# A newly written order of all engines for a windowed attention and rational MoE kernel on one core

## The chip, the core and the metric

The kernel runs on one core of one Trainium2 chip. The metric is the device time of one execution in microseconds (us), lower is better. Runs of the same kernel on one chip agree within some 0.3%.

## The reference, cut to what matters

Attention over 8 batches and 8 heads of 576 positions (head size 64) with two masks, and behind it a two-layer network whose activation is a quotient of polynomials:

```python
mask_plain = (rel >= 0) & (rel < window)
mask_dil = (rel >= 0) & (rel < window * dilation) & (rel % dilation == 0)
...
scores = np.where(masks[None, :, :, :], scores, -1000000000.0)
scores = scores - np.max(scores, axis=-1, keepdims=True)
attn = np.exp(scores)
attn = attn / (np.sum(attn, axis=-1, keepdims=True) + 1e-09)
return np.matmul(attn, v).astype(np.float32)
...
h = x @ w_in
P = a[0] + a[1] * h + a[2] * h2 + a[3] * h3
Q = 1.0 + np.abs(b[0]) * np.abs(h) + np.abs(b[1]) * h2
g = P / (Q + 1e-06)
return (g @ w_out).astype(np.float32)
```

There are 4608 tokens of width 512 and 2048 hidden units, all in float32.

## The kernel before, in words

The attention is cut into 48 units of six per batch (`Unit`, U0 to U47), the network into tiles (`Tile`, T0 to T111, and from T112 on `QuadTile`): a tile is 128 hidden units (f) by 512 tokens (a column block c). What the tensor engine multiplies is held as a high and a low float32r part.

**A unit** does its scores on PE; then on DVE mask, maximum and subtraction, on ACT the exponential, on DVE a 32x32 transposition (`turn`, L561). From there it goes through memory: SP issues `put` (L575, the profile's turned<-u), waits until that has landed, and issues `move` (L569, two transfers, the profile's pT<-turned). Then one step on PE, the unit's use (the profile's pair), multiplies by v and does the scores of the unit two further on. The loads of qk and v are issued by SP too. The results are normed and turned on DVE (`turn_out`) and become the high and low parts xh and xl of a block's tokens; the last 64 tokens of each batch go to memory instead (left<-y).

**A tile** is one step h on PE (12 matmuls into one of two PSUM banks; 4 full float32 ones for T0 to T5), a chain (`plan_chain`, L1029) of three ACT steps on h, a product a<-r,a called qq (L1037, DVE or POOL), two DVE steps t1 and t2, ln and exp on ACT, three DVE steps g0, g1, g2, then the high part gh (L1050: ACT, DVE or POOL) and the low part gl (L1051: DVE or POOL), and four steps out on PE of three matmuls each. The bank is free when g2 is done, so h of a tile waits for g2 of the tile two before it.

**Sums and Mix** prepare the last two column blocks, which are multiplied with seven products in place of eight (`Quad`). `Mix.fetch` (L1389, the profile's left<-left) reads what the units' left<-y wrote to memory, and `Mix.one` (L1400, the profile's t<-left,xh) is the first that uses it.

**The order is written out by hand.** Each piece of work is an operation with a number. `Plan.run` (L324) walks through the list ISSUE (L78) and emits the operations in that order; an operation goes to the engine that the table ENGINE (L236) gives for its number, and without an entry to the first engine that it allows. The list holds 3929 steps, and each engine has its own steps in the list's order: PE 813, DVE 1279, ACT 1017, POOL 434, SP 386. An engine never passes a step that waits. In the list a unit's turn, put, move and use have the numbers 534, 535, 536, 555 for U22, and 424, 425, 426, 445 for U15.

Of the kernel before, what the change touches and what calls it, by code (L numbers as in the profile page):

```python
# [97 lines left out]
    1144, 1145, 204, 197, 406, 1142, 407, 1143, 408, 1147, 1146, 409, 1148, 1155, 1132, 203, 1156, 1157, 1158, 1159, 1162, 1163, 1160, 1161, 1164,
    1117, 1115, 1116, 205, 1165, 1166, 209, 1080, 238, 240, 159, 239, 241, 1078, 1118, 1133, 1149, 1150, 206, 1173, 1174, 1175, 1177, 1135, 1136,
    1134, 1176, 227, 400, 1178, 199, 1179, 228, 1167, 1168, 1180, 1181, 1183, 1182, 1184, 229, 200, 201, 1191, 1192, 1194, 1193, 1151, 1152, 1154,  # L100
    1153, 1209, 1169, 1172, 1171, 1170, 401, 1196, 211, 244, 274, 220, 262, 232, 410, 1195, 246, 242, 1185, 1186, 1198, 1199, 1197, 1201, 1200, 1202,
    222, 1210, 234, 1211, 1212, 1213, 1216, 1217, 1214, 1215, 1218, 1219, 1220, 230, 207, 1203, 212, 1204, 1227, 245, 221, 1187, 1190, 1228, 1230,
    1229, 252, 233, 223, 1231, 1232, 247, 213, 1189, 1188, 1221, 1222, 1234, 1235, 1233, 1236, 1237, 1245, 248, 251, 1246, 1247, 1248, 1249, 253, 235,
    1238, 236, 224, 254, 1207, 1205, 1206, 1208, 1263, 1226, 1224, 1223, 1250, 1239, 1252, 1253, 225, 237, 231, 1240, 255, 276, 243, 1251, 1255, 1254,
    1256, 412, 427, 256, 280, 268, 398, 396, 411, 1225, 1244, 1242, 1281, 1243, 1241, 269, 1264, 1266, 257, 1265, 1257, 1268, 1267, 263, 1270, 1271,
    1269, 1258, 258, 264, 1282, 1284, 281, 1273, 1272, 259, 265, 1274, 1275, 270, 1276, 1261, 1259, 1260, 1299, 1262, 1278, 1279, 1283, 275, 282,
    1285, 249, 1288, 1289, 260, 1286, 1287, 1291, 1290, 1302, 1300, 1301, 1304, 1292, 1305, 1293, 1294, 271, 261, 1303, 1306, 1307, 1277, 1280, 1317,
    1297, 1298, 1295, 1296, 1309, 1308, 1310, 266, 1318, 1320, 1319, 1322, 1321, 1323, 267, 1335, 1311, 1312, 1324, 1325, 272, 277, 278, 273, 1327,
    1326, 1328, 1314, 1316, 1315, 1353, 1313, 1336, 1337, 1338, 1329, 402, 1339, 1342, 1343, 1330, 279, 1340, 1341, 1344, 1345, 1346, 1354, 1355,
    1347, 403, 1356, 1357, 283, 284, 1360, 414, 1331, 415, 420, 416, 1358, 1348, 1359, 421, 417, 422, 1361, 1363, 1362, 1332, 1379, 1380, 1334, 1333,  # L110
    429, 1351, 1382, 423, 418, 1384, 1364, 424, 1381, 1383, 1386, 1387, 436, 1385, 430, 1388, 1389, 1365, 1366, 285, 1397, 1350, 1349, 1352, 1368,
    1370, 1369, 1398, 1400, 1399, 1401, 1404, 419, 404, 431, 1390, 432, 433, 1377, 1405, 1391, 1402, 1403, 437, 434, 1392, 1367, 1415, 1373, 1375,
    1371, 438, 1406, 1407, 1408, 443, 435, 439, 1416, 1417, 1418, 413, 425, 426, 445, 440, 452, 453, 1376, 454, 428, 441, 442, 1378, 444, 1394, 1393,
    1395, 1396, 1433, 1420, 1419, 446, 1409, 455, 456, 1421, 1410, 1422, 1423, 1424, 1425, 1426, 1436, 1434, 1435, 1438, 447, 1427, 1414, 1412, 1411,
    1437, 1440, 1441, 1439, 448, 1442, 1443, 1444, 1372, 1428, 1413, 1451, 1432, 1430, 1431, 457, 458, 1374, 459, 475, 451, 1452, 1454, 1456, 1457,
    461, 1429, 468, 462, 1469, 1453, 1455, 1445, 1458, 1459, 1460, 1446, 1461, 1462, 1463, 1464, 1470, 1472, 1471, 449, 469, 463, 464, 1473, 1476,
    1477, 470, 1474, 1475, 1479, 1478, 1480, 1450, 1447, 1449, 1448, 1487, 1466, 477, 1465, 1468, 1505, 1467, 1488, 1489, 1481, 471, 1491, 1490, 1494,
    465, 1495, 1482, 450, 466, 1483, 1485, 478, 479, 480, 484, 472, 1492, 1493, 481, 1496, 1508, 1506, 485, 1497, 1498, 486, 1484, 1486, 473, 1523,
    474, 491, 460, 1526, 467, 1529, 1507, 1510, 1509, 1512, 1513, 1499, 1511, 1514, 1500, 1515, 482, 1535, 493, 1538, 1536, 1537, 1539, 1503, 1502,
    1501, 1516, 1517, 499, 500, 1540, 1518, 1541, 1542, 1543, 1544, 1553, 1504, 501, 1545, 494, 1521, 1519, 1556, 1554, 502, 1555, 1557, 1520, 1558,  # L120
    1546, 1524, 1522, 1527, 1559, 1530, 1571, 1547, 1548, 1532, 476, 1528, 1533, 495, 1525, 492, 506, 1531, 483, 1560, 487, 1561, 521, 1550, 1551,
# [1542 lines left out]
```

## Time and profile before

| | |
|---|---|
| Median of 3 runs | 930.32 us (929.02 to 931.96) |
| The profiled execution | 929.68 us, its span 927.9 us |
| Granted clock of PE over the span | 0.985 |
| PE, DVE, ACT, POOL busy | 95%, 87%, 70%, 54% |

The profile names an instruction by line, engine and tiles (out<-in). Almost all are issued by small helpers, so that the line tells little and the tiles tell the work. PE is the tensor engine's matmuls, DVE the vector engine, ACT the scalar engine, POOL the GpSimd engine, SP the queue that issues the transfers.

### The profile page before, as it was taken

The numbers are of one execution on the slowest core, as the hardware profiler recorded it, in microseconds if no ns is written. First come the engines' busy times: TensorE is split into PE (matmuls) and PEld (weight loads), VectorE is DVE, ScalarE is ACT, GpSimd is POOL, SyncE is SP. The second block draws the span as 40 slices with busy tenths as digits, with TensorE's granted clock in tenths as the row PEclk, the third lists the DMA queues.
The fourth block names the chain that finished last, engine by engine and source line by source line (L and its number), as shares of the span: only waits on it lengthen the run. The fifth ranks groups of instructions, "written<-read, shape, count | busy, mean of one in ns | idle before, by whom it ended". The sixth has DMA issues, their size and how long they took to land.

```text
span 927.9 us, 20345 instructions
## 1 busy us (share of the span) xinstructions
PE 879.9 (95%) x7788; PEld 690.8 (74%) x7788; DVE 809.8 (87%) x1447; ACT 651.5 (70%) x1042; POOL 503.4 (54%) x460
## 2 busy tenths in 40 slices
PE   8799998989999999899799999999897999999998
PEld 6346876867777787787678887877685888877786
DVE  6899997988988799889788799899987889999886
ACT  5698897755677566656577676766775778988761
POOL 3476876732445434257567654576773665544650
PEclk9899999999999999999899999999999999999999
DMA  9988550034353433234564066117563035355023
GB/s 336 282 264 278 181 201 0 16 81 118 119 176 88 116 114 115 80 111 123 144 194 146 1 191 189 35 40 239 161 181 109 1 103 147 125 174 186 5 91 137
DMA packets 93634, 125.20 MB, mean 135 GB/s; under 512 B 39648, under 2 KB 64864, under 8 KB 93024
## 3 DMA queue, kind: packets, MB, share of 16 engines
q1 hardware_dynamic: 93248, 123.80, 42.2%
q8 instruction: 61, 1.00, 0.4%
q14 instruction: 37, 0.30, 0.1%
q10 hardware_dynamic: 288, 0.10, 0.1%
HBM read 86.25 MB, written 37.62 MB: 133 GB/s over the span
## 4 chain that ended last, share of the span: by engine, by line
PE 45%; DVE 24%; DMA 10%; ACT 8%; issue 6%; POOL 4%; SPq 2%; DVEq 0%; POOLq 0%; ACTq 0%
PE out L367 21%; PE h L367 14%; ACT r L370 5%; DVE h L376 4%; DVE a L376 4%; PE pair L367 3%; SPq L364 2%; DMA turned<-u 2%; PE hy L367 2%; DMA pT<-turned 2%; DVE t L373 2%; PE hz L367 2%; PE hx L367 2%; DVE a L373 2%; DMA qk<-in_qk_dram 2%
## 5 line engine op out<-in xcount | busy, mean ns | idle before, releaser
L367 PE MATMUL out<-gh,wo 128*128 128x512 f32 x1104 | 346.7, 395 | 0.0
L367 PE MATMUL h<-xh,wi 128*128 128x512 f32 x848 | 284.4, 396 | 12.6 <-DVE a L376 12.1
L367 PEld LDWEIGHTS out<-gh,wo 128*128 128x128 f32 x1104 | 206.8, 190 | 44.9 <-ACT os L370 0.7
L367 PE MATMUL out<-gl,wo 128*128 128x512 f32 x552 | 216.7, 393 | 1.0 <-POOL gl L379 0.9
L367 PEld LDWEIGHTS h<-xh,wi 128*128 128x128 f32 x848 | 160.2, 189 | 55.0 <-DVE a L376 19.7
L379 POOL TENSOR_TENSOR a<-r,a 128x512 f32<-128x512 f32 x68 | 89.5, 1316 | 177.6 <-ACT r L370 157.0
L367 PE MATMUL h<-xl,wi 128*128 128x512 f32 x424 | 166.0, 391 | 0.0
L379 POOL TENSOR_TENSOR gl<-a,gh 128x512 fp32r<-128x512 f32 x92 | 125.1, 1360 | 36.7 <-DVE gh L382 19.6
L370 ACT ACTIVATE r<-a,ln_bias 128x512 f32<-128x512 f32 x112 | 80.8, 722 | 76.1 <-POOL a L379 42.0
L367 PEld LDWEIGHTS out<-gl,wo 128*128 128x128 f32 x552 | 104.6, 189 | 24.3 <-POOL gl L379 2.1
L370 ACT ACTIVATE t<-h,na_t 128x512 f32<-128x512 f32 x112 | 86.1, 769 | 30.2 <-PE h L367 27.4
L370 ACT ACTIVATE r<-r,exp_bias 128x512 f32<-128x512 f32 x144 | 104.0, 722 | 4.1
L370 ACT ACTIVATE r<-a,ab_t 128x512 f32<-128x512 f32 x112 | 91.2, 814 | 21.3 <-DVE a L376 14.1
L370 ACT ACTIVATE a<-h 128x512 f32<-128x512 f32 x112 | 66.3, 592 | 53.4 <-PE h L367 42.0
L376 DVE SCALAR_TENSOR_TENSOR h<-h,na_t,r 128x512 f32<-128x512 f32 x112 | 84.1, 751 | 16.4 <-ACT r L370 15.0
L373 DVE TENSOR_TENSOR t<-t,h 128x512 f32<-128x512 f32 x112 | 75.8, 676 | 24.8 <-ACT t L370 14.8
L376 DVE SCALAR_TENSOR_TENSOR a<-a,r 128x512 f32<-128x512 f32 x112 | 88.4, 790 | 7.1 <-ACT r L370 6.0
L367 PEld LDWEIGHTS h<-xl,wi 128*128 128x128 f32 x424 | 80.2, 189 | 16.2 <-issue 0.5
L376 DVE SCALAR_TENSOR_TENSOR h<-t,na_t,h 128x512 f32<-128x512 f32 x112 | 83.7, 748 | 1.9
L376 DVE SCALAR_TENSOR_TENSOR a<-a,h 128x512 f32<-128x512 f32 x106 | 72.1, 680 | 2.6
L391 POOL TENSOR_SCALAR gh<-a 128x512 fp32r<-128x512 f32 x37 | 27.1, 733 | 56.3 <-PE out L367 29.6
L379 POOL TENSOR_TENSOR place<-r,place 128x512 f32<-128x512 f32 x26 | 35.0, 1351 | 39.9 <-ACT r L370 39.1
(207 smaller groups left out, 1361.5 us busy)
## 6 DMA issues: line engine op xcount, KB each, us to landing
qk<-in_qk_dram SPq DMA_DIRECT2D x48, 448.0 KB, 4.8
v<-in_vp_dram SPq DMA_DIRECT2D x48, 390.0 KB, 4.3
out_dram<-os SPq DMA_DIRECT2D x36, 256.0 KB, 3.0
wi_raw<-in_w_in_dram SPq DMA_DIRECT2D x16, 512.0 KB, 5.3
wo_raw<-in_w_out_dram SPq DMA_DIRECT2D x16, 512.0 KB, 6.0
turned<-u SPq DMA_DIRECT2D x42, 192.0 KB, 2.1
pT<-turned SPq DMA_DIRECT2D x84, 96.0 KB, 2.7
sums<-wi SPq DMA_DIRECT2D x24, 256.0 KB, 3.0
```

The costliest lines, as they stand in the source:

```text
L364: pin((nc.scalar if eng == "ACT" else nc.sync).dma_start(dst, src))
L367: pin(nc.tensor.matmul(o, lhs, rhs, start=start, stop=stop, skip_group_check=skip))
L370: pin(nc.scalar.activation(o, i, func, **kw))
L373: pin(nc.vector.tensor_tensor(o, x, y, op))
L376: pin(nc.vector.scalar_tensor_tensor(o, x, s, y, op0, op1))
L379: pin(nc.gpsimd.tensor_tensor(o, x, y, op))
L391: pin(nc.gpsimd.tensor_scalar(o, x, 1.0, 0.0, ALU.mult, ALU.add))
```

## The change

The first 240 steps of ISSUE stay as they are (the last PE step among them is h of T3, at 49 us of the span). From there on the 3689 others stand in a new order, on every engine. No operation is added or taken away. Of those that stand on the same engine before and after, 606 of PE's 813 have another place in PE's order (by 1.8 places in the mean, 18 at most), and 301 of SP's 386 (2.6 and 12).

The table ENGINE names another engine for 259 operations. Two of these, 0 and 3, have no effect: their functions pass the queue "ACT" themselves (L1220, L1238). Of the 257 others 72 go from DVE to POOL, 69 from POOL to DVE, 41 from ACT to POOL, 32 from POOL to ACT, 26 from DVE to ACT and 17 from ACT to DVE. Of the products qq, 28 come to DVE and 18 leave it; of the low parts gl, 10 come and 18 leave.

The core of the diff: the lines with U22's turn, put, move and use, those with the first step of Mix (3138), and two of ENGINE's.

```diff
@@ -83,206 +83,209 @@
...
-    1654, 1655, 1662, 1664, 1663, 1665, 1668, 1669, 1666, 540, 546, 1667, 541, 542, 1656, 1679, 1640, 1641, 543, 1680, 1682, 1658, 1671, 1670, 1672,
-    534, 528, 544, 547, 1673, 1681, 1683, 1659, 1697, 1674, 1684, 548, 549, 550, 1685, 1686, 1687, 1688, 522, 538, 545, 553, 535, 536, 569, 1689, 555,
...
-    2806, 2826, 2807, 2824, 2828, 2829, 2830, 2831, 3138, 2834, 2835, 2832, 2833, 2836, 2837, 2838, 3139, 3137, 3145, 3140, 2846, 2848, 3142, 2847,
...
+    529, 1635, 1636, 528, 532, 1622, 1623, 520, 1646, 1645, 1648, 1624, 1661, 1621, 533, 1637, 1647, 534, 1649, 1638, 1650, 1651, 1640, 1639, 1662,
+    1664, 1653, 1652, 1654, 1663, 1665, 539, 1666, 1655, 1668, 1667, 535, 522, 553, 536, 569, 1656, 1669, 1679, 1641, 1642, 546, 547, 540, 541, 542,
+    1670, 1682, 543, 1680, 545, 1658, 1671, 544, 1672, 1657, 1673, 1684, 1685, 1697, 1681, 1674, 1683, 548, 549, 550, 1675, 1700, 1698, 1686, 1687,
+    1676, 1660, 555, 1659, 1678, 1677, 1702, 551, 538, 1689, 1688, 1690, 1699, 1715, 1701, 1691, 562, 563, 556, 557, 1704, 1705, 564, 565, 1703, 1706,
...
+    941, 2832, 2833, 934, 2837, 2836, 2838, 942, 3135, 3136, 2846, 2847, 2848, 2849, 2852, 2853, 2850, 2851, 2839, 2840, 2855, 3138, 2854, 2856, 2863,
...
 ENGINE = {
-    12: "ACT", 24: "ACT", 36: "ACT", 49: "ACT", 55: "ACT", 63: "ACT", 69: "ACT", 78: "ACT", 84: "DVE", 86: "ACT", 87: "DVE", 88: "ACT", 89: "DVE",
...
+    0: "SP", 3: "SP", 12: "ACT", 24: "ACT", 36: "ACT", 49: "ACT", 55: "ACT", 63: "ACT", 69: "ACT", 78: "ACT", 84: "DVE", 86: "ACT", 87: "DVE",
```

What the lists put between a unit's put and its use can be counted. The table gives the PE steps that stand in the list between the step that lets SP issue the put (the unit's turn, or, where that stands later, the step on another engine that an earlier entry of SP's queue waits for) and the use. "out0" is an out of T0 to T5, with full float32 matmuls.

| Unit | before | after |
|---|---|---|
| U15 | 1 h, 1 out | 1 h, 7 out |
| U18 | 1 h, 2 out | 3 h, 11 out, 1 use |
| U19 | 1 h, 4 out | 3 h, 9 out |
| U22 | 1 h, 1 out | 2 h, 9 out, 1 use |
| U29 | 1 h, 3 out | 2 h, 7 out |
| U33 | 5 out | 1 h, 5 out, 1 use |
| U35 | 1 h, 5 out | 2 h, 8 out |
| U39 | 1 h, 5 out | 2 h, 9 out, 1 use |
| U11 | 2 h, 7 out0, 1 use | 1 h, 2 out0, 1 use |
| U20 | 2 h, 6 out, 1 use | 1 h, 5 out |
| U27 | 3 h, 10 out, 1 use | 1 h, 5 out |
| U45 | 2 h, 7 out | 2 h, 10 out |

In DVE's order the first step of Mix (3138) stands 5 steps behind turn_out of U47 before and ahead of t1, t2, g0, g1 and g2 of T102 (2832 to 2838); after, it stands 13 steps behind that turn_out, behind all of T102's steps, and ahead of g0 and g2 of T103 (2854, 2856).

## Rows read from the trace of the kernel before

**Rows 1.** The page's first part: busy time and share by engine.
```profile
PE 879.9 (95%) x7788; PEld 690.8 (74%) x7788; DVE 809.8 (87%) x1447; ACT 651.5 (70%) x1042; POOL 503.4 (54%) x460
```

**Rows 2.** Windows from 50 us: PE, PEld, DVE, ACT, POOL busy; clock, DMA share, GB/s.
```profile
50.00:125.00 75.00, 74.50 (x814) 49.41 (x813) 72.93 (x138) 65.16 (x110) 57.50 (x51) 1.00 0.78 261
125.00:200.00 75.00, 71.16 (x490) 57.02 (x489) 67.58 (x108) 59.03 (x95) 51.69 (x45) 1.00 0.11 28
200.00:450.00 250.00, 236.52 (x2633) 190.15 (x2632) 218.31 (x417) 158.72 (x252) 109.72 (x101) 0.98 0.39 114
450.00:475.00 25.00, 19.74 (x261) 15.55 (x260) 17.84 (x39) 14.51 (x26) 10.49 (x11) 0.86 0.73 221
475.00:650.00 175.00, 174.01 (x1572) 140.72 (x1570) 155.15 (x280) 121.90 (x191) 110.07 (x97) 1.00 0.40 122
650.00:690.00 40.00, 37.02 (x429) 29.30 (x429) 37.32 (x75) 29.73 (x49) 30.50 (x30) 1.00 0.52 165
690.00:725.00 35.00, 28.55 (x119) 22.83 (x119) 25.89 (x40) 22.61 (x34) 15.84 (x13) 0.95 0.37 107
725.00:900.00 175.00, 173.60 (x761) 141.86 (x760) 158.25 (x236) 142.97 (x224) 94.09 (x79) 1.00 0.34 110
```

**Rows 3.** Waits of PE from 50 us on: us in total, times, longest.
```profile
PE pair L367 <- DMA pT<-turned: 12.4, 8, 4.9
PE h L367 <- DVE a L376: 12.1, 11, 4.8
PE pair L367 <- DMA qk<-in_qk_dram: 3.0, 2, 2.1
PE pair L367 <- DMA v<-in_vp_dram: 2.2, 2, 1.4
```

**Rows 4.** The window behind U33's wait, columns as in the windows above.
```profile
462.00:464.00 2.00, 2.00 (x73) 1.64 (x61) 0.90 (x3) 0.00 (x0) 0.00 (x0) 0.50 0.77 235
```

**Rows 5.** The page's DMA issues: count, KB each, median us to landing.
```profile
qk<-in_qk_dram SPq DMA_DIRECT2D x48, 448.0 KB, 4.8
...
turned<-u SPq DMA_DIRECT2D x42, 192.0 KB, 2.1
pT<-turned SPq DMA_DIRECT2D x84, 96.0 KB, 2.7
```

**Rows 6.** The chain in order of time, steady stretches of PE: start, us, what.
```profile
45.73 3.43 PE out L367 x8
...
168.40 2.72 PE h L367 x12
171.12 2.72 PE out L367 x12
```

**Rows 7.** PE's timeline, a unit's use (pair) and the step behind it.
```profile
188.70 0.67 PE L367 MATMUL pair<-v,pT 64*32 64x65 f32 x44
...
189.83 0.73 PE L367 MATMUL out<-gh,wo 128*128 128x512 f32 x2
```

**Rows 8.** Timelines of DVE and SP about the first step of Mix.
```profile
692.78 0.68 DVE L373 TENSOR_TENSOR a<-r,a 128x512 f32<-128x512 f32 x1
699.33 0.69 DVE L373 TENSOR_TENSOR t<-left,xh 128x512 f32<-128x512 f32 x1 [5.87 <-DMA sums<-wi]
...
690.04 0.88 SPq L364 DMA_DIRECT2D left<-y  x2
...
693.36 0.81 SPq L364 DMA_DIRECT2D left<-left  x2
```

**Rows 9.** Groups of DVE and POOL: count, busy us, mean ns, idle before.
```profile
L376 DVE SCALAR_TENSOR_TENSOR a<-a,r 128x512 f32<-128x512 f32 x112 | 88.4, 790 | 7.1 <-ACT r L370 6.0 <-POOL gl L379 1.1
...
L376 DVE SCALAR_TENSOR_TENSOR a<-a,h 128x512 f32<-128x512 f32 x106 | 72.1, 680 | 2.6
L373 DVE TENSOR_TENSOR a<-r,a 128x512 f32<-128x512 f32 x44 | 38.2, 868 | 5.6 <-ACT r L370 5.1 <-POOL wo L379 0.4
...
L379 POOL TENSOR_TENSOR a<-r,a 128x512 f32<-128x512 f32 x68 | 89.5, 1316 | 177.6 <-ACT r L370 157.0 <-DVE t L373 12.8 <-PE pair L367 5.2
```

More of the change, by code (lines that the diff above doesn't have):

```diff
@@ new lines @@
+    108: "POOL", 110: "POOL", 111: "POOL", 114: "ACT", 116: "POOL", 117: "POOL", 120: "ACT", 122: "ACT", 123: "POOL", 126: "POOL", 128: "POOL",
+    129: "DVE", 132: "POOL", 134: "ACT", 135: "DVE", 138: "POOL", 140: "ACT", 141: "POOL", 144: "ACT", 146: "POOL", 147: "POOL", 150: "ACT",
+    152: "POOL", 153: "DVE", 156: "POOL", 158: "ACT", 159: "POOL", 162: "ACT", 164: "ACT", 165: "POOL", 168: "POOL", 170: "DVE", 171: "POOL",
+    174: "POOL", 176: "ACT", 177: "POOL", 180: "POOL", 182: "ACT", 183: "POOL", 186: "ACT", 188: "ACT", 189: "POOL", 192: "ACT", 194: "ACT",
@@ new lines @@
+    195: "POOL", 198: "ACT", 200: "POOL", 201: "POOL", 204: "POOL", 206: "POOL", 207: "POOL", 210: "POOL", 212: "ACT", 213: "DVE", 216: "POOL",
+    218: "ACT", 219: "POOL", 222: "ACT", 224: "ACT", 225: "POOL", 228: "ACT", 230: "ACT", 231: "POOL", 234: "POOL", 236: "POOL", 237: "POOL",
+    240: "POOL", 242: "POOL", 243: "POOL", 246: "ACT", 248: "ACT", 249: "DVE", 252: "POOL", 254: "DVE", 255: "POOL", 258: "POOL", 260: "DVE",
+    261: "DVE", 264: "ACT", 266: "POOL", 267: "POOL", 270: "POOL", 272: "ACT", 273: "DVE", 276: "ACT", 278: "ACT", 279: "POOL", 282: "ACT",
@@ new lines @@
+    284: "POOL", 285: "POOL", 312: "DVE", 327: "POOL", 342: "POOL", 388: "DVE", 404: "DVE", 419: "POOL", 434: "POOL", 466: "POOL", 498: "DVE",
+    513: "POOL", 528: "DVE", 560: "POOL", 592: "DVE", 607: "POOL", 622: "POOL", 654: "DVE", 670: "DVE", 686: "POOL", 701: "POOL", 716: "POOL",
+    780: "POOL", 795: "POOL", 810: "DVE", 826: "POOL", 874: "POOL", 889: "POOL", 904: "POOL", 934: "DVE", 947: "DVE", 963: "POOL", 979: "POOL",
+    995: "POOL", 1011: "POOL", 1027: "DVE", 1043: "POOL", 1051: "ACT", 1052: "POOL", 1061: "POOL", 1069: "POOL", 1070: "POOL", 1075: "ACT",
@@ new lines @@
+    1077: "DVE", 1079: "ACT", 1081: "ACT", 1087: "DVE", 1095: "DVE", 1096: "POOL", 1105: "DVE", 1113: "POOL", 1114: "POOL", 1123: "DVE", 1131: "ACT",
+    1132: "POOL", 1141: "DVE", 1149: "ACT", 1150: "POOL", 1159: "DVE", 1167: "ACT", 1168: "POOL", 1177: "DVE", 1185: "ACT", 1186: "POOL", 1195: "DVE",
+    1203: "POOL", 1204: "POOL", 1213: "DVE", 1221: "POOL", 1222: "POOL", 1231: "DVE", 1239: "ACT", 1240: "POOL", 1249: "DVE", 1257: "ACT",
+    1258: "DVE", 1267: "DVE", 1275: "POOL", 1276: "POOL", 1285: "POOL", 1293: "POOL", 1294: "POOL", 1303: "POOL", 1311: "POOL", 1312: "POOL",
@@ new lines @@
+    1321: "DVE", 1329: "ACT", 1330: "POOL", 1339: "DVE", 1347: "ACT", 1348: "POOL", 1357: "POOL", 1365: "POOL", 1366: "POOL", 1371: "ACT",
+    1373: "ACT", 1375: "ACT", 1377: "ACT", 1383: "POOL", 1391: "ACT", 1392: "DVE", 1401: "POOL", 1409: "POOL", 1410: "POOL", 1419: "DVE", 1427: "DVE",
+    1428: "POOL", 1437: "POOL", 1445: "POOL", 1446: "POOL", 1455: "POOL", 1463: "ACT", 1464: "POOL", 1473: "POOL", 1481: "POOL", 1482: "POOL",
+    1491: "POOL", 1499: "POOL", 1500: "POOL", 1509: "POOL", 1517: "DVE", 1518: "POOL", 1539: "POOL", 1547: "POOL", 1548: "POOL", 1557: "POOL",
@@ new lines @@
+    1565: "DVE", 1566: "POOL", 1575: "POOL", 1583: "DVE", 1584: "POOL", 1593: "DVE", 1601: "ACT", 1602: "POOL", 1619: "POOL", 1709: "DVE",
+    1710: "DVE", 1719: "POOL", 1727: "ACT", 1737: "POOL", 1745: "POOL", 1763: "POOL", 1764: "POOL", 1781: "POOL", 1791: "DVE", 1799: "POOL",
+    1817: "ACT", 1823: "ACT", 1825: "ACT", 1827: "DVE", 1829: "ACT", 1843: "DVE", 1853: "DVE", 1861: "ACT", 1879: "POOL", 1880: "DVE", 1897: "DVE",
+    1915: "POOL", 1925: "DVE", 1933: "POOL", 1943: "DVE", 1951: "POOL", 1961: "DVE", 1969: "POOL", 1979: "DVE", 1987: "DVE", 1988: "POOL",
@@ new lines @@
+    3056: "POOL", 3060: "DVE", 3061: "POOL", 3062: "POOL", 3063: "POOL", 3064: "POOL", 3065: "POOL", 3066: "DVE", 3067: "POOL", 3070: "POOL",
+    3071: "POOL", 3075: "POOL", 3076: "POOL", 3077: "POOL", 3078: "POOL", 3079: "POOL", 3080: "DVE", 3081: "ACT", 3082: "POOL", 3085: "ACT",
+    3086: "POOL", 3090: "POOL", 3091: "DVE", 3092: "POOL", 3093: "DVE", 3094: "POOL", 3095: "DVE", 3096: "POOL", 3097: "POOL", 3100: "DVE",
+    3101: "POOL", 3105: "POOL", 3106: "POOL", 3107: "POOL", 3108: "POOL", 3109: "POOL", 3110: "POOL", 3111: "POOL", 3112: "POOL", 3115: "POOL",
@@ new lines @@
+    3116: "DVE", 3120: "POOL", 3121: "POOL", 3122: "POOL", 3123: "DVE", 3124: "POOL", 3125: "POOL", 3126: "ACT", 3127: "POOL", 3130: "ACT",
+    3131: "DVE", 3138: "DVE", 3139: "POOL", 3140: "ACT", 3141: "POOL", 3142: "ACT", 3143: "POOL", 3144: "DVE", 3145: "DVE", 3146: "ACT", 3147: "DVE",
+    3148: "ACT", 3149: "POOL", 3150: "POOL", 3151: "POOL", 3152: "POOL", 3153: "DVE", 3157: "DVE", 3158: "POOL", 3159: "ACT", 3160: "DVE",
+    3161: "POOL", 3162: "DVE", 3163: "POOL", 3164: "POOL", 3165: "POOL", 3166: "DVE", 3167: "POOL", 3168: "DVE", 3169: "POOL", 3170: "POOL",
@@ new lines @@
+    3171: "ACT", 3172: "POOL", 3214: "POOL", 3240: "POOL", 3281: "POOL", 3307: "POOL", 3308: "DVE", 3337: "POOL", 3350: "POOL", 3376: "POOL",
+    3377: "DVE", 3404: "POOL", 3405: "POOL", 3417: "POOL", 3418: "DVE", 3431: "DVE", 3465: "DVE", 3473: "POOL", 3499: "POOL", 3500: "DVE",
+    3540: "POOL", 3558: "DVE", 3566: "POOL", 3733: "ACT", 3735: "ACT", 3737: "ACT", 3739: "ACT", 3773: "ACT", 3775: "DVE", 3777: "DVE", 3779: "ACT",
+    3899: "POOL", 3900: "POOL", 3901: "POOL", 3902: "POOL", 3903: "POOL", 3904: "DVE", 3905: "POOL", 3906: "POOL", 3907: "POOL", 3910: "ACT",
@@ L286 @@
+    3912: "ACT", 3913: "ACT", 3914: "POOL", 3916: "ACT", 3917: "ACT", 3918: "POOL", 3920: "DVE", 3921: "DVE", 3922: "POOL", 3924: "ACT", 3925: "ACT",
+    3926: "POOL", 3928: "ACT",
 }
```

61 lines of the change are left out of this document (13 added, 48 removed), and 290 rows, old and new, of the table ISSUE.

## The prediction

> **What bounds the kernel now.** I read the busy shares first: PE is busy for 879.9 us of a span of 927.9, 95% [rows 1]. Nothing in the change alters what PE multiplies, so PE's work stays, and all that can go is its idle time and the time at a low clock. Then the windows, for where these lie [rows 2]. Idle time is the window less PE's busy time: 0.5 us in 50 to 125, 3.8 in 125 to 200, 13.5 in 200 to 450, 5.3 in 450 to 475, 1.0 in 475 to 650, 3.0 in 650 to 690, 6.4 in 690 to 725, 1.4 in 725 to 900. The three windows with the most are also the only ones with a granted clock under 1: 0.98, 0.86 and 0.95 of full speed. Full speed lost to it is (1 - 0.98) * 250 = 5.0 us, 0.14 * 25 = 3.5 and 0.05 * 35 = 1.75. Then PE's waits, for who ends the idle time [rows 3]: after 50 us a unit's use waits 12.4 us for the transfer pT, 3.0 for qk and 2.2 for v, together 17.6 us in 12 waits, and h waits 12.1 us in 11 for g2 on DVE. A low clock comes with a long wait: behind the longest, 4.9 us, PE works at 0.50, the lower of its two levels, 1.2 of 2.4 GHz [rows 4].
>
> So transfers that land late cost PE their wait and often a slow stretch behind it. The longest wait for DVE belongs to them too: at 693.5 us DVE reaches the first step of Mix and stands for 5.87 us until left<-left has landed [rows 8], with T102's whole chain queued behind it, and h of T104 waits 4.8 us for that chain [rows 3].
>
> **The change, part by part.**
>
> *The way of a unit through memory.* From the turn, the put takes 2.1 us and the move 2.7 to land [rows 5], 4.8 in all, about 5.5 with a turn of some 0.7 (an estimate: the DVE steps shown take 0.68 to 0.87, [rows 9]). Against that stands the PE work between, from the step counts in the section on the change: an h is 2.72 us, an out 2.72 / 4 = 0.68, a full float32 out 3.43 / 4 = 0.86 [rows 6], a use 189.83 - 188.70 = 1.13 [rows 7]. Before, that gives 3.4 us for U15 and U22, 3.4 for U33, 4.1 for U18, 4.8 for U29 and 5.4 for U19, and these are the smallest six of the units after 50 us; the next, U35 and U39, have 6.1. All the waits for pT and nearly all of those for qk and v lie at those six, at U27 and U45, and at U16, whose qk was issued late. After, the six have 7.5, 12.7, 7.2, 16.8, 10.2 and 14.3. The smallest of all are then U11 with 5.6 and U20 and U27 with 6.1. By this count the class that waits is empty, and of the 17.6 us some 15 should go; U11 and U45, below, keep the rest.
>
> *From 200 to 475.* Idle 13.5 + 5.3 = 18.8 and clock 5.0 + 3.5 = 8.5, together 27.3 us. How much stays can be bounded by stretches without such waits: 475 to 650 leaves PE 1.0 us idle of 175, 0.6%; 125 to 200 leaves 3.8 of 75, 5.1%, all of it h waiting for DVE [rows 2]. On 275 us these are 1.6 and 14.0. DVE's work over PE's is 218.3 / 236.5 = 0.92 in 200 to 450, more than the 0.89 of 475 to 650 and less than the 0.95 of 125 to 200. I take 11 left, nearer the upper end, since waits that are gone leave DVE less time to catch up: **-16 us**, between -13 and -26.
>
> *Mix, 650 to 725.* Idle 9.4 and clock 1.75, 11.2 us. The write and the read of left take from 690.04 to 699.3, 9.3 us [rows 8]. Before, DVE had 5 steps for it and stood still for 5.87. After it has 13 steps of about 0.7, 9.1 us, with the whole of T102's chain among them, so its wait should nearly vanish, and with it most of the 6.4 us of idle time and the slow clock. What is late next is g0 and g2 of T103, which now stand right behind the step of Mix, and U45's use (2 h and 10 out, 12.2 us, but SP issues other transfers between). I leave 4 us: **-7**, between -3 and -11.
>
> *The busy queue, 50 to 125.* The 16 DMA engines are 78% busy there [rows 2]. U11's cover falls from 2 * 2.72 + 7 * 0.86 + 1.13 = 12.6 us to 2.72 + 1.72 + 1.13 = 5.6 (U10's falls too). Where transfers crowd, the medians of 2.1 and 2.7 don't hold: U33's wait of 4.9 us lies in a stretch with a DMA share of 0.73 [rows 2, 3]. No row prices it; from below nothing, from above one wait as long as the longest, with its slow clock, 4.9 + 3.5 = 8.4. I take **+3**, nearer nothing, since only one or two of the units there are under 9 us.
>
> *The quiet stretches, 125 to 200, 475 to 650 and 725 to 900.* Their order is new as well, and they idle 3.8 + 1.0 + 1.4 = 6.2 us of 425. At 0.6% they would have 2.6, at 5.1% 22. Most are near the lower end now, so a new order has more to lose than to gain: **+3**, between -4 and +12.
>
> *Copies and adds on other engines.* 98 steps leave DVE and 86 come. The products qq are 868 ns on DVE and 1316 on POOL [rows 9]: 10 more on DVE is +8.7 us there, and 22 other steps leave it, 15 us at 0.68. DVE's 809.8 us then change by some -6 us. POOL gets 113 and gives 101, under 20 us on 503 at 1.3 each; it has 46% idle. I price this at nothing: the cover is POOL's idle time, and if it is gone, gl comes late and out waits for it. No step of SP is added; 301 of its steps are moved, but few by much, and PE's waits above price that.
>
> Here a row speaks against moving work between these two. On DVE a<-a,r, both operands in SBUF, takes 790 ns in the mean, and a<-a,h, one of them in PSUM, 680 [rows 9]: something holds the first back, by 0.11 * 112 = 12.3 us in all, and by the same comparison the 44 products by 0.188 * 44 = 8.3. If that grows with POOL's work, by 2%, it is 0.4 us; if each of the 10 products that come is held as those are, the 868 ns already hold it. The Trainium skill, SBUF — State Buffer, "Who interferes with whom", says that a DVE instruction with two SBUF inputs contends with a GpSimd instruction that reads SBUF; by that rule the moves could cost up to a whole POOL step for each meeting, without it they are free. The rows agree in direction; no row tells how often steps meet after the change.
>
> The sum: -16 - 7 + 3 + 3 = -17 us on the profiled execution's 929.68 us, which stands 0.64 under the median: 930.32 - 17 = 913.3, so **913 us**.
>
> **The rivals.**
>
> *Everything goes.* The stretches to 475 come down to 0.6% idle, Mix is clean, nothing new: -26 - 10 - 2 = -38, some 892 us; from -29 on, under 901, I count it here. For it: 475 to 650 has units and tiles of the same kind and reaches that share. Against it: DVE is at 0.92 of PE's work there. Chance 0.10.
>
> *The time is given back.* The transfers no longer wait, but DVE had used those pauses: h waits instead, at the upper share of 5.1% everywhere new. 27.3 - 14.0 = 13.3 and 3 come, 12 + 3 go: about 929 us, from 925 to 933. For it: where DVE has 0.95 of PE's work, PE did lose 5.1%. Chance 0.14.
>
> *Slower: DVE takes the place of the transfers.* An h that now waits for g2 costs 12.1 / 11 = 1.1 us each [rows 3]; with a slow stretch behind every second of them (1.75 us each, as in 690 to 725) 2 us. If more than some ten new ones come beyond the 11 of today, on top of the upper share, the change loses: 20 new ones, one in five tiles, cost 40 us against the 23 saved, 947 us. A step of DVE that a POOL step holds back lengthens that very chain. Counted in the two lists, from the end of the last PE step that an h hangs on through any queue: h steps with at most 5.0 us of PE work in between are 18 before and 17 after, which speaks against it. For it: single tiles get much closer (T80 from 8.6 us to 2.0, T64 from 5.2 to 2.7), and the count is weak, since T104 waited 4.8 us with 8.8 before. Chance 0.11, with times from 933 up.
>
> That the change doesn't do what it says holds for 2 of its 259 entries alone; it has no chance of its own.
>
> **How the numbers follow.** My forecast, 901 to 925, has 0.65; the three rivals 0.10, 0.14 and 0.11. A measurement of this kernel can tell about 0.3% from no change, 2.8 us, so faster is under 927.5. Of the case that gives the time back a third or so is faster, 0.05, the rest, 0.09, the same. Faster is 0.65 + 0.10 + 0.05 = 0.80, same 0.09, slower 0.11. The range from 901 to 930 leaves out 0.11 above, about 0.04 of the same, and 0.05 of the tail below.
>
> **What would show it.** In the changed profile PE's waits for pT, qk and v after 50 us should fall from 17.6 us to under 4, and the 450 to 475 and 690 to 725 windows should have a clock of 1.00. DVE should wait less than 1 us at t<-left,xh. The waits of h for DVE should stay under 15 us. The forecast is wrong if those waits for transfers stay, which is a fault of the count in the lists, or if they go and h's waits for DVE or out's for gl grow by as much, which is the second or third rival. A wait at U10 or U11, near 80 us, longer than 3 us would be the busy queue's price put too low.

## The result, and the profile after

The changed kernel takes 891.03 us (median of 4 runs, 890.46 to 893.49) against 930.39; the ratio is 0.9581, with a 95% interval from 0.9558 to 0.9605. The prediction said 913 us with a range from 901 to 930. The direction was right, the size was not: the gain is 39 us and not 17, and the time lies where the rival "everything goes" had it (892).

The first part of the page of the changed kernel (span 889.2 us, granted clock 0.996), to be read beside [rows 1]:

```profile
PE 868.2 (98%) x7788; PEld 684.1 (77%) x7788; DVE 798.7 (90%) x1436; ACT 648.8 (73%) x1042; POOL 511.6 (58%) x471
```

PE does the same 7788 matmuls in 11.7 us less, some 10 of them by the clock (a mean of 0.985 over 927.9 us loses 13.9, 0.996 over 889.2 loses 3.6), and the other 27.0 of the 38.7 us between the spans are idle time. Windows of the changed kernel, columns as in [rows 2]. Their ends are put where PE has done the same sum of work as at 50, 125, 200, 450, 475, 650, 690, 725 and 900 us before (the matmul times of the steps, added up in the order of each list):

```profile
50.00:126.30 76.30, 75.52 (x814) 49.10 (x813) 74.89 (x142) 64.63 (x111) 51.61 (x48) 1.00 0.66 221
126.30:197.30 71.00, 70.26 (x490) 57.23 (x489) 66.30 (x110) 58.20 (x93) 49.70 (x40) 1.00 0.21 71
197.30:428.90 231.60, 231.07 (x2639) 187.42 (x2637) 213.78 (x413) 160.32 (x256) 120.95 (x111) 1.00 0.42 127
428.90:445.70 16.80, 16.80 (x268) 13.56 (x254) 16.22 (x38) 11.22 (x20) 11.22 (x11) 1.00 0.64 194
445.70:617.90 172.20, 171.90 (x1588) 140.06 (x1594) 152.42 (x279) 122.29 (x192) 107.40 (x97) 1.00 0.41 123
617.90:657.80 39.90, 38.22 (x434) 29.89 (x420) 38.84 (x73) 28.66 (x49) 26.55 (x25) 1.00 0.62 190
657.80:685.10 27.30, 26.62 (x118) 21.38 (x116) 24.38 (x37) 21.94 (x34) 17.68 (x15) 1.00 0.43 132
685.10:861.30 176.20, 174.38 (x762) 142.15 (x763) 162.81 (x239) 141.79 (x222) 94.96 (x82) 1.00 0.34 109
```

Read each row's first two numbers: from 197 to 446 us PE is idle for 0.5 us in 248, where it was 18.8 in 275, and no window has a clock under 1.00. All of PE's waits from 50 us on, beside [rows 3]:

```profile
PE h L370 <- DVE a L379: 3.6, 9, 0.7
PE hx L370 <- DVE a L379: 1.2, 1, 1.2
PE out L370 <- ACT os L373: 1.0, 1, 1.0
PE h L370 <- DVE g L379: 0.6, 1, 0.6
```

Not one transfer is left in it, and h's waits for DVE have fallen from 12.1 to 3.6 us as well. That second fall is what the prediction did not expect. Mix's first step, beside [rows 8], now starts without a wait, between steps of T103:

```profile
668.88 0.69 DVE L379 SCALAR_TENSOR_TENSOR a<-a,r 128x512 f32<-128x512 f32 x1 [0.16 <-ACT r L373]
669.49 0.68 DVE L376 TENSOR_TENSOR t<-left,xh 128x512 f32<-128x512 f32 x1
670.09 0.75 DVE L379 SCALAR_TENSOR_TENSOR h<-h,na_t,r 128x512 f32<-128x512 f32 x1
```

The gain by stretch, at equal PE work, for the changed kernel and for five of the runs below (us gained on the profile of before; the columns are named as the runs are told below; a single profile varies by some 3 us, since the same wait of a unit is sometimes followed by a stretch at the low clock, a slow stretch below, and sometimes not; where the order is new, the bounds between two rows are good to 1 or 2 us):

| Stretch of before, us | forecast | changed | transfers alone | new front | stretch 1 | two stretches | two, old table |
|---|---|---|---|---|---|---|---|
| 0 to 50 | 0 | -0.1 | -0.2 | 0.1 | 0.4 | 0.4 | 1.2 |
| 50 to 125 | -3 | -1.2 | 0.1 | -1.2 | 0.1 | 0.1 | -4.3 |
| 125 to 200 | quiet | 4.0 | 0.0 | 4.0 | 3.9 | 3.9 | -4.1 |
| 200 to 475 | 16 | 26.6 | 22.8 | 26.6 | 3.0 | 22.0 | 21.5 |
| 475 to 650 | quiet | 2.8 | 0.1 | -4.0 | -0.4 | 3.4 | -6.7 |
| 650 to 725 | 7 | 7.8 | -0.9 | -0.1 | -1.1 | 8.6 | -3.7 |
| 725 to end | quiet | -1.2 | -1.0 | -1.7 | -0.3 | -3.5 | -23.4 |
| sum | 17 | 38.7 | 20.9 | 23.7 | 5.6 | 34.9 | -19.5 |

The three quiet stretches together were forecast at -3 and gave 5.6.

### The profile page after: what moved, and what is told of

Same layout as the page of the kernel before. It is cut to its first block, busy times and chain, and to the rows that moved or that the text cites. A ratio compares the mean times of both kernels' runs of the same rounds, so it can differ in the third digit from the quotient of the medians.

```text
span 889.2 us, 20368 instructions
## 1 busy us (share of the span) xinstructions
PE 868.2 (98%) x7788; PEld 684.1 (77%) x7788; DVE 798.7 (90%) x1436; ACT 648.8 (73%) x1042; POOL 511.6 (58%) x471
## 4 chain that ended last, share of the span: by engine, by line
PE 65%; DVE 21%; DMA 5%; issue 4%; ACT 4%; POOL 1%; SPq 0%; DVEq 0%; ACTq 0%; POOLq 0%
PE out L370 31%; PE h L370 22%; DVE a L379 5%; DVE h L379 4%; PE pair L370 4%; PE hx L370 2%; PE hy L370 2%; PE hz L370 2%; ACT r L373 2%; DVE a L376 2%; DVE t L376 2%; DVE pair L376 1%; DMA turned<-u 1%; DMA pT<-turned 1%; PE hv L370 1%
## 5 line engine op out<-in xcount | busy, mean ns | idle before, releaser
L370 PE MATMUL out<-gh,wo 128*128 128x512 f32 x1104 | 343.1, 392 | 1.0 <-ACT os L373 1.0
L382 POOL TENSOR_TENSOR gl<-a,gh 128x512 fp32r<-128x512 f32 x97 | 134.1, 1383 | 55.6 <-ACT gh L373 29.8
L382 POOL TENSOR_TENSOR a<-r,a 128x512 f32<-128x512 f32 x54 | 70.3, 1301 | 123.3 <-ACT r L373 105.1
L382 POOL TENSOR_TENSOR place<-r,place 128x512 f32<-128x512 f32 x30 | 39.9, 1329 | 44.8 <-ACT r L373 38.6
L394 POOL TENSOR_SCALAR gh<-a 128x512 fp32r<-128x512 f32 x48 | 34.5, 718 | 46.3 <-PE out L370 24.1
```

The source lines that it names most:

```text
L370: pin(nc.tensor.matmul(o, lhs, rhs, start=start, stop=stop, skip_group_check=skip))
L382: pin(nc.gpsimd.tensor_tensor(o, x, y, op))
L394: pin(nc.gpsimd.tensor_scalar(o, x, 1.0, 0.0, ALU.mult, ALU.add))
```

## The experiments

In the lists below a line is a part of one engine's own order, by the operations' numbers. Each ratio is to runs of the kernel before that were made beside it (medians from 927.2 to 928.8 us).

### Order without table, table without order

The new order with the old table:

```diff
-    1105: "DVE", 1123: "DVE",
+    1105: "POOL", 1123: "POOL",
...
```

> The new order with the old table of engines. Theory O, the order carries all of it and the engine moves are free, as the prediction priced them: 889 to 894 us, h waiting under 6 us for DVE after 50 us. Theory E, the 11 us that DVE's busy time lost (809.8 to 798.7 us) are why h no longer waits, so that the prediction's 11 us left in 200 to 475 and 3 us in the quiet stretches went by the table: DVE back near 810 us busy, h waiting 12 us or more, 900 to 907 us. Theory M, order and table were made for each other and either alone is worse than that: over 910 us.

1004.29 us, ratio 1.0811 (1.0779 to 1.0842). And the old order with the new table:

> The old order with the new table of engines. Theory M, order and table were made for each other: well slower than before, 945 us or more, with h waiting for DVE and out for gl and gh all over, as the new order with the old table was 8% slower than before. Theory E, the table lightens DVE by itself: 915 to 930 us.

1030.18 us, ratio 1.1089 (1.1056 to 1.1121). Theory M holds in both. Neither half is worth anything by itself: they are 76 and 103 us slower than before, while the two together are 39 faster. PE's waits of the first, from 50 us on:

```profile
PE h L367 <- DVE a L376: 37.3, 34, 3.1
PE out L367 <- POOL gl L379: 8.8, 11, 1.9
PE out L367 <- DVE gl L373: 6.7, 5, 5.0
```

The second's list begins with the same three, 38.2, 7.2 and 7.2 us. DVE is busy for 828.0 and 824.7 us, 18 and 15 more than before, which is not 76 and 103: it stands still among its work. My reading is that the order decides when a step may start and the table how long its queue is held, so that one changed without the other puts steps behind others that are not ready; these two runs alone don't show it, and two such places are looked at in a trace below.

### One engine's order put back

The next three put the old order of some engines back into the changed kernel; SP's, as an example, around U15:

```diff
 SP:
-413, 443, 425, 459, 1376, 426
+443, 435, 413, 425, 426, 1376
```

> The changed kernel with SP's order put back as near to the old one as the dependencies allow (578 of 644 exchanged pairs undone); the other four engines and the table as changed. Theory C, the transfers' cover is what counts and SP's order sets most of it: by the count U15's put and v have 1.4 us of PE work, v of U29 0, qk at U16 0, at U25 0.7 and at U34 5.4, against 5.5 us needed, some 4 + 5.5 + 5 + 4 us of waits and two to four slow stretches of 1.75: 905 to 916 us. Theory T, the place of turn and use decides and SP only follows: under 896 us.

953.13 us, ratio 1.0266 (1.0245 to 1.0287). From 50 us on:

```profile
PE pair L370 <- DMA pT<-turned: 13.1, 8, 5.0
PE pair L370 <- DMA qk<-in_qk_dram: 8.7, 2, 7.1
PE h L370 <- DVE a L379: 6.8, 7, 4.3
```

The transfers' waits are back (21.8 us, 17.6 before), as theory C had it, but the time is 37 us over its range: a place in a queue chosen for one order is late in another.

> The changed kernel with PE's order put back (925 of 937 exchanged pairs undone), everything else as changed. Theory C: by the count only v at U12 (0 us), U41 (4.8) and qk at U29 and U45 are under 5.5 us, 2 to 8 us of waits with their slow stretches: 893 to 901 us, h waiting for DVE as short as now. Theory P, PE's order is what gives DVE's chains their time, since h stands later behind the tile two before it: h's waits for DVE return, 10 us or more, 902 to 912 us.

1004.05 us, ratio 1.0801 (1.0764 to 1.0837): above both theories; uses wait 17.5 us for the tile y on DVE, h 16.4 for g2.

> The changed kernel with the orders of DVE, ACT and POOL put back as far as the dependencies allow (1699 of 1826, 993 of 1129 and 370 of 380 exchanged pairs undone); PE's, SP's and the table as changed. Mix's first step stands 6 places behind turn_out of U47 again, ahead of T102's steps. Theory C with the prediction's Mix term: covers stay (only U29 with 4.8 and U45 with 4.1 us are under 5.5), Mix's wait of some 6 us on DVE and its 7 us come back, with 1 to 2 us for U29 and U45: 898 to 902 us, all of it in 640 to 700. Theory D, DVE's own order is why h no longer waits: waits of h for DVE also in 125 to 475, 10 us or more, 905 to 915 us.

1104.77 us, ratio 1.1898 (1.1871 to 1.1925): h waits 77.5 us for DVE, and both theories are far off. The misses say one thing: putting one queue back tells the price of a mismatch, not what that queue's order had gained. The edits that follow are therefore small ones, to the kernel before.

### The transfers alone

```diff
 SP:
-435, 413, 425, 426
+413, 425, 426, 435
-444, 1372, 457, 458, 1374, 459, 475
+459, 444, 1372, 457, 458, 1374, 475
-473, 1523, 474, 491, 460
+491, 460, 473, 1523, 474
-521, 1534, 489, 490
+1534, 489, 490, 521
-630, 645, 646, 1828, 655, 639, 632, 1826, 663
+630, 632, 663, 645, 646, 1828, 655, 639, 1826
-3043, 725, 695, 3039, 707, 3042, 708
+695, 725, 707, 3043, 708, 3039, 3042
-3102, 3113, 895, 3117, 883
+3102, 883, 3113, 895, 3117
 PE:
-555, 1660, 1657, 1676, 1678
+1660, 1657, 1676, 1678, 555
-915, 2708, 2773
+2708, 2773, 915
```

(U22's use stands four outs later, not five.) 425, 426 and 707, 708 are put and move of U15 and U33; 413, 460, 632, 695 and 883 load v; 459, 491, 521, 663 and 725 load qk.

> The kernel before, with transfers alone moved ahead in SP's queue (put and move of U15, put of U33, and loads of v or qk for U15, U16, U18, U29, U33, U45; one load of qk behind the move of U19), and two uses moved back on PE (U22's by five outs, U45's by an out and an h); table, DVE, ACT and POOL as before. Theory R, the prediction's residue: waits for pT, qk and v fall from 17.6 to under 5 us, but h waits for DVE instead, some 11 us of the 27 in 200 to 475 stay: 913 to 918 us with U45's. Theory F, DVE was never behind it: all of it goes, h's waits stay near 12 us, 902 to 908 us. Theory M, every change of one queue alone upsets the others, as undoing one did: no faster than 925 us.

908.59 us, ratio 0.9783 (0.9754 to 0.9812). That is 0.6 us above theory F's range and 4 below theory R's, and the waits below are those of theory F. This is the run that decides the prediction's largest term. All of PE's waits in the stretch that was 200 to 475, before:

```profile
PE pair L367 <- DMA pT<-turned: 9.8, 7, 4.9
PE pair L367 <- DMA qk<-in_qk_dram: 3.0, 2, 2.1
PE pair L367 <- DMA v<-in_vp_dram: 2.2, 2, 1.4
PE pair L367 <- DVE h L376: 1.7, 1, 1.7
PE h L367 <- DVE a L376: 1.2, 1, 1.2
PE pair L367 <- DVE y L610: 0.6, 1, 0.6
```

and the same stretch (200 to 452.3 us) with the transfers moved:

```profile
PE h L367 <- DVE a L376: 1.4, 2, 1.2
PE pair L367 <- DVE y L610: 0.6, 1, 0.6
PE pair L367 <- DMA pT<-turned: 0.5, 2, 0.3
```

With every step of DVE, ACT and POOL where it was and the old table, h waits 1.4 us for DVE where it waited 1.2. DVE did not need the pauses. Its windows say the same: 2.6 us idle, clock 1.00.

```profile
200.00:434.30 234.30, 231.71 (x2635) 186.26 (x2634) 215.99 (x418) 158.58 (x252) 110.10 (x101) 1.00 0.42 125
434.30:452.30 18.00, 18.00 (x260) 14.36 (x259) 17.50 (x39) 14.89 (x26) 10.50 (x11) 1.00 0.78 232
```

So 22.8 of the 26.6 us of that stretch, and over half of the whole change, are had by thirteen entries moved in SP's queue and one use on PE (883 and 915 belong to U45, behind that stretch).

At U45 it went otherwise. Its wait of 2.6 us is gone too, but in 650 to 725 h now waits 8.0 us for DVE in 7 times where it waited 6.8 in 4 (new at T99, T100 and T103, 2.0 us together), and the stretch gained nothing (-0.9). There the pause was given back, as the second rival says. DVE's work over PE's is 37.32 / 37.02 = 1.01 in 650 to 690 of [rows 2], against 0.92 in 200 to 450.

### The quiet stretch by hand

Why does h wait for DVE in 125 to 200? Five weight copies stand in front of two chains' last steps (1238, 1274):

```diff
 DVE:
-247, 1233, 1236, 1237, 253, 235, 1238
+1233, 1236, 1237, 1238, 247, 253, 235
-259, 265, 1274
+1274, 259, 265
```

> The kernel before, with five weight copies moved on DVE alone: wi 11 to 13's and wo 12's behind the last chain step (g2) of T16, wi 14's and wo 13's behind g2 of T18. Theory F, the h waits of 125 to 200 us, from which the prediction took its 5.1% for DVE, are an accident of the old order: the waits at h of T18 (1.5 us) and T20 (1.4) go, PE idles under 1.5 us in 125 to 200 (3.8 before), and the time falls by 2 to 3 us (ratio 0.997 to 0.998). Theory L, DVE's load is the limit there: the waits move to the next tiles and the time stays (ratio 0.999 to 1.001).

934.37 us, ratio 1.0056 (1.0035 to 1.0078): slower, which neither theory had. The h waits nearly go, as theory F says, but another comes. PE's waits between 90 and 200 us:

```profile
PE out L367 <- POOL gl L379: 4.6, 1, 4.6
PE h L367 <- DVE a L376: 0.8, 2, 0.6
```

and POOL's timeline there:

```profile
146.15 1.30 POOL L379 TENSOR_TENSOR a<-r,a 128x512 f32<-128x512 f32 x1 [5.76 <-ACT r L370]
147.41 0.62 POOL L391 TENSOR_SCALAR wi<-wi_f 128x512 fp32r<-128x512 f32 x1
148.00 0.62 POOL L391 TENSOR_SCALAR gh<-a 128x512 fp32r<-128x512 f32 x1
148.58 2.96 POOL L379 TENSOR_TENSOR wi<-wi_f,wi 128x512 fp32r<-128x512 f32 x2
151.51 1.26 POOL L379 TENSOR_TENSOR wo<-wo_f,wo 128x512 fp32r<-128x512 f32 x1
152.73 1.26 POOL L379 TENSOR_TENSOR gl<-a,gh 128x512 fp32r<-128x512 f32 x1
```

The out waits for a gl that stands on POOL behind three weight copies, and these stand behind a product that waits 5.76 us for ACT, where it waited 3.73 before. ACT has a weight copy of its own in its queue, of a wi_f that DVE now does later. ACT's timeline at that copy, before and under it with DVE's copies moved:

```profile
142.19 0.63 ACT L370 ACTIVATE wi<-wi_f 128x512 fp32r<-128x512 f32 x1 [0.22 <-DVE wi_f L376]
```

```profile
143.48 0.63 ACT L370 ACTIVATE wi<-wi_f 128x512 fp32r<-128x512 f32 x1 [2.74 <-DVE wi_f L376]
```

The three ACT steps on the next tile's h, with the r that POOL's product needs, stand behind it. With gl of T16 put ahead of POOL's copies too:

```diff
 POOL:
-225, 237, 231, 1240
+1240, 225, 237, 231
```

> The five weight copies moved on DVE as in the run with them alone, and on POOL the low part gl of T16 moved ahead of three weight copies (wi 11, wi 12, wo 10). There the h waits went, but PE reached out of T16 sooner and stood 4.6 us for that gl, which came no earlier. Theory Q, waits travel along in-order queues, and with both queues mended they are gone: no wait of out for gl near 150 us, 2 to 3.5 us faster (ratio 0.996 to 0.998). Rival: DVE or POOL is short of time there, and a third wait follows: ratio 0.999 or more.

932.12 us, ratio 1.0061 (1.0037 to 1.0085). The wait for gl falls to 0.6 us, and h waits for DVE again, 4.3 us in 4 (3.2 in 3 before), mostly at T19 to T21: a third wait follows, as the rival says. Its reason, that DVE or POOL is short of time there, isn't shown, for ACT still stands 2.75 us at its weight copy, which neither edit moved. By hand the wait was only pushed from queue to queue.

### Mix by hand

```diff
 DVE:
-3138, 2832, 2833, 2836, 2837, 2838, 2850
+2832, 2833, 2836, 2837, 2838, 2850, 3138
```

> The kernel before, with Mix's first step moved on DVE behind t1, t2, g0, g1, g2 of T102 and t1 of T103 (six ACT steps that hang on it move along), nothing else. Theory X, the prediction's term for Mix: DVE waits under 1 us for left<-left, h of T104 no longer waits 4.8 us, the slow stretch at 703 us goes, 5 to 8 us faster (ratio 0.991 to 0.995). Rival Y, the wait only moves: h of T105 or T106 waits instead, since T103's steps and Mix's own follow at once: ratio 0.998 to 1.002.

928.12 us, ratio 0.9984 (0.9967 to 1.0001): no difference that can be told, as rival Y has it. DVE's wait is nearly gone (0.37 us) and so is the slow stretch, but look at the second numbers of DVE's timeline:

```profile
701.67 0.69 DVE L373 TENSOR_TENSOR t<-left,xh 128x512 f32<-128x512 f32 x1 [0.37 <-DMA sums<-wi]
702.45 1.83 DVE L373 TENSOR_TENSOR left<-b,left 128x512 f32<-128x512 f32 x1
704.20 1.77 DVE L373 TENSOR_TENSOR a<-r,a 128x512 f32<-128x512 f32 x1
...
706.55 1.17 DVE L382 CAST gh<-a 128x512 fp32r<-128x512 f32 x1
...
708.43 1.78 DVE L376 SCALAR_TENSOR_TENSOR a<-a,r 128x512 f32<-128x512 f32 x1
```

Three steps with both operands in SBUF take 1.8 us in place of 0.7 (the second of them, a<-r,a, took 1.77 before as well), and h of T105 waits 1.9 us and out of T102 1.8, for gh on DVE, together 3.7 of the 6.4 us that h waited there before. More than half of the wait moved.

The three edits in one kernel:

> The kernel before with the edits of the three runs before this one together, some 70 of its 3929 steps, and the old table of engines. If waits add up (theory F): 893 to 900 us, nearly the changed kernel's 891, so that the table and the other 3600 moved steps bring little. If they do not (theory R or L): the sum falls short of the three single gains by over 5 us.

909.08 us, ratio 0.978 (0.9756 to 0.9804): as the transfers alone, neither reading. And with gl of T16 moved on POOL as well, and Mix's steps in an order nearer to the new one:

```diff
 DVE:
-3138, 2832, 2833, 2836, 2837, 2838, 2850, 3144, 2849, 2851, 2839, 2840, 2855, 2854, 2856
+2832, 2833, 2836, 2837, 2838, 2839, 2840, 2849, 2850, 2851, 2855, 3138, 2854, 2856, 3144
```

> The kernel before with the transfers' edits, the copies on DVE and gl on POOL, and at Mix its first step on DVE behind the chain of T102 and g1 of T103, with gh and gl of T102 ahead of T103's steps and Mix's third step behind g2 of T103; the old table. If these waits add up: 20.2 for the transfers, 2 to 3 for the copies, 3 to 6 for Mix: 898 to 903 us. If Mix's stretch needs the new table (DVE's steps there were held back to 1.8 us each by POOL): 904 to 907 us.

906.93 us, ratio 0.9776 (0.9744 to 0.9809). The time is in the second range: what the transfers left is not had by moving these few steps. That it needs the new table is not shown here; the last two runs bear on it.

### Order and table together, stretch by stretch

The first 2144 steps new, order and table, the rest old:

> New order and new table together up to the 2144th step (500 us of the span before), from there on the old order with the old table. The two lists have all but one step in common up to there. Theory A, order and table work as a pair, stretch by stretch, and the gains of stretches add up: the trace of the changed kernel was 28.7 us ahead at that point, so 899 to 902 us. Rival: the seam breaks the back part as the seams between engines did: over 910 us.

906.41 us, ratio 0.9765 (0.9737 to 0.9794). At 500 us its trace is 28.9 us ahead of before, the changed kernel's 28.7; behind the seam the old part loses 4 us that it did not lose before, at h of T94 (2.0 us and a slow stretch). The time lies between the two ranges: the front gains what theory A says, the seam costs as the rival says, but less.

Then stretch 1, the steps 440 to 893 alone, with the 41 entries of the table that belong to them, and without:

> The kernel before with the new order of the steps 440 to 893 (90 to 195 us, 453 steps) and the new table's 41 entries for them; all else old. Theory A, a stretch of the new order and table works by itself: the 4 us that the changed kernel gained from 100 to 200 us, ratio 0.995 to 0.997, h of T18 and T20 waiting under 1 us together (2.9 before). Rival: the gain hangs on what stands ahead or behind, ratio 0.999 or more.

922.91 us, ratio 0.9936 (0.9915 to 0.9958).

> The same new order of the steps 440 to 893 with the old table throughout. Theory O, the order of that stretch carries its gain and the 41 entries nothing: as the run with them, ratio 0.995 to 0.998. Theory M, an order is only good with the table that it was written for: slower than before, ratio 1.003 or more.

940.89 us, ratio 1.0134 (1.0101 to 1.0166). Theory A holds (the time is a little under its range), and theory M. The first gains the 3.9 us of the changed kernel in that stretch, h waiting 0.7 us (the 3.0 that it gains in 200 to 475, where nothing was moved, are slow stretches that did not come); the second loses 8.4 in it. Forty-one entries are worth some 12 us there (18 in the whole time), and only with their order. How they can act, two of them show, though no run has these two alone: qq of T9 and T10 (1105, 1123) are on DVE in the new table and on POOL in the old. DVE with the old table, at g0 and g1 of T9 and g0 of T10:

```profile
104.05 0.72 DVE L376 SCALAR_TENSOR_TENSOR h<-h,na_t,r 128x512 f32<-128x512 f32 x1
104.68 1.79 DVE L376 SCALAR_TENSOR_TENSOR a<-a,r 128x512 f32<-128x512 f32 x1
...
110.36 0.76 DVE L376 SCALAR_TENSOR_TENSOR h<-h,na_t,r 128x512 f32<-128x512 f32 x1 [1.79 <-ACT r L370]
```

and POOL beside it:

```profile
104.63 1.28 POOL L379 TENSOR_TENSOR wo<-wo_f,wo 128x512 fp32r<-128x512 f32 x1
107.52 1.30 POOL L379 TENSOR_TENSOR a<-r,a 128x512 f32<-128x512 f32 x1 [1.60 <-ACT r L370]
```

T10's qq takes 1.30 us on POOL in place of 0.80, comes later, ln and exp come later, and DVE stands for 1.79 us at g0 with everything behind it queued. And a<-a,r at 104.68 meets a POOL step and takes 1.79. DVE's group in 90 to 195 us, old table, and under it the new one:

```profile
L376 DVE SCALAR_TENSOR_TENSOR a<-a,r 128x512 f32<-128x512 f32 x16 | 15.2, 953 | 0.4 <-ACT r L370 0.4
```

```profile
L376 DVE SCALAR_TENSOR_TENSOR a<-a,r 128x512 f32<-128x512 f32 x18 | 14.2, 789 | 1.0 <-ACT r L370 1.0
```

This mean is 809 ns in the kernel before and 829 in the changed one in the same window, so that fewer meetings are not where the changed kernel's gain came from; more of them are a part of what the old table costs with the new order.

Last, two stretches: the transfers' edits in the middle, and new order and table in 90 to 195 and 593 to 793 us, then the same with the old table:

> The kernel before with the new order and table in the steps 440 to 893 and 2543 to 3355 (90 to 195 and 593 to 793 us), and between them the transfers' edits for U15 to U33 on the old order and table. Theory A, what the transfers left lies in these two stretches and the gains add up: 908.6 - 4 - 7.5 and some, 893 to 898 us. Rival: the seams give back several us each, as at 607 us in the run with a new front: 900 to 906 us.

894.68 us, ratio 0.9636 (0.9613 to 0.9659): theory A, the gains add up. In 650 to 725 the 8.6 us that Mix by hand did not bring are there.

> The same order with the old table throughout. Theory O: as the run with the table's 108 entries for the two stretches, 893 to 900 us. Theory M: both stretches fall behind the old order, over 912 us, with h waiting for DVE and out for gl in them.

949.95 us, ratio 1.0234 (1.0212 to 1.0257): the same order without the 108 entries is 55 us slower. Theory M. What is left between 894.7 and 891 lies, by the table above, in 200 to 475 and behind 725.

## Why the prediction was right and wrong

**The transfers' count was right.** All six units with under 5.5 us of cover stopped waiting once they had 7 or more, U27 and U20 with 6.1 and U11 with 5.6 don't wait either, and the run with the transfers alone shows that the cover is the cause. The waits for transfers went to nothing (forecast: under 4 us) and the slow stretches with them, as the count and [rows 3, 4] said. In the sum some 1.4 us of the 27.3 stand twice: in the last 2.8 us of U33's wait PE stands still and the granted clock is already 0.50, so that they are counted as idle and as clock.

**The step that failed is "I take 11 left" in 200 to 475.** Measured is 0.5 us in the changed kernel, and 2.6 in the run where DVE kept its old order and table. The 5.1% came from another stretch, 125 to 200, on the argument that waits that are gone leave DVE less time to catch up. Nor were its 3.8 us "all of it h waiting for DVE": 2.9 were, and 0.9 was an out waiting for gl on POOL. A nearer row is h's waits for DVE in 200 to 475 themselves, 1.2 us in one. A DVE at 0.92 of PE's work did not hold PE up there; after the change it is at 0.93 (213.78 / 231.07) with nothing lost. The argument itself is not empty: at U45, with the transfers alone, the pause was given back. This term is 10.6 of the 21.7 us by which the sum was off.

**"The quiet stretches, +3" had the wrong sign,** 5.6 us gained, 8.6 of the error. 125 to 200 was not at its limit: the stretch with new order and table gains 3.9 us by itself, with h waiting 0.7 us. The five copies moved by hand don't show this, since there the wait came back on other queues. **The busy queue, +3,** was 1.2, inside its bounds; U10 and U11 do not wait, with 78% of the DMA engines' time taken before and 66% after. **Mix, -7,** measured 7.8, but the working behind it was incomplete: putting its step later was counted as the whole. Done alone it gave nothing that can be told: gh of T102 and T105's h were late next, which the prediction named only in part (g0 and g2 of T103).

**"Copies and adds on other engines: nothing" was the wrong kind of term.** As a number in a sum it can't be tested: the table without the order is 103 us slower, the order without the table 76, in two stretches alone 55. The sum treated 259 entries as a load (DVE -6 us, POOL +20); what they seem to do, by the two places shown above, is to place a step where its queue is free at that moment. DVE's busy time did fall, by 11.1 us, but most of the gain comes without that: with the transfers alone and in the run of two stretches it fell by 4.1 (to 805.7), and these are 20 and 34 us faster. The cost set against it, steps held back where DVE and POOL meet, did not grow. The changed kernel's groups, beside [rows 9]:

```profile
L379 DVE SCALAR_TENSOR_TENSOR a<-a,r 128x512 f32<-128x512 f32 x112 | 89.5, 799 | 6.3 <-ACT r L373 5.5 <-POOL gl L382 0.7
...
L376 DVE TENSOR_TENSOR a<-r,a 128x512 f32<-128x512 f32 x58 | 46.5, 802 | 6.7 <-ACT r L373 6.3 <-POOL place L382 0.2
```

The mean of the first is 799 ns for 790, of the products on DVE, 58 for 44, 802 for 868.

**The rivals.** "Everything goes" came out with 892 against 891. In part that is luck: its terms of 26, 10 and 2 measured 26.6, 7.8 and 5.6, and 1.2 was lost in 50 to 125. It had a chance of 0.10 for "DVE is at 0.92 there", the same argument as above; and since it holds all that is under 901, the 0.05 that the range leaves out below is too little by the prediction's own count. "Time given back" and "DVE takes over" are seen nowhere in the changed kernel; the first is seen at U45 with the transfers alone, the second in the mismatched kernels (h waiting 16 to 78 us for DVE in all but the one with SP's old order), so both are real, and this order with its table avoids them.

## What to carry to other kernels

Price what may take over in a stretch by rows of that stretch, not by a share of another one: here 1.2 us of waits stood against a borrowed 11. Such waits are a lower bound and no more. In 200 to 475 they were the whole (1.4 us with the transfers alone); with the copies or Mix moved by hand, waits came out that had been 0.9 us or none before (4.6 for gl, 1.8 for gh). Where queues run in a written order, placing a step on another engine and ordering it are one decision; costing them apart, or testing one without the other, gives the price of a mismatch (1 to 19% slower than before here), not the share of the gain. What could be had by hand was in the transfers: where a use waits for one, its entry moved up in the queue that issues it, with two uses moved back on PE, brought 20 of the 39 us.

## What the runs showed of the hardware

Steps of DVE of 128x512 with both operands in SBUF take 0.68 us alone and up to 1.8 beside a POOL step (1.79 at 104.68 us above, where POOL's own step takes 1.28); the chain's steps with an operand in PSUM keep their 0.68 to 0.76 (none of the 106 a<-a,h of before takes over 0.69). The Trainium skill, SBUF — State Buffer, "Who interferes with whom", has DVE and GpSimd share one pair of ports that one of them locks, so that a step can lose up to the other's whole duration; 0.68 + 1.28 is 1.96, and the 1.79 agree. What was not expected is how much of this the choice of engines can cause in one and the same order, with nearly the same number of POOL steps (62 and 61): 789 against 953 ns for one group in one stretch.

A wait of PE is not always followed by a stretch at the lower clock. In the run with stretch 1 alone PE works at full speed behind its waits for U22 (1.7 us) and U29 (1.5 us), where the profile of before has a clock of 0.50 behind waits of 1.7 and 1.4 us at the same units. A forecast should carry this part of a gain as a range: in this kernel it is up to 10.25 us (5.0 + 3.5 + 1.75) in one execution, some 1.4 of them while PE stands in U33's wait.
